# Local/global attention with routed experts: where an even block leaves, when weights split, how list entries are sent

## The chip, the cores and the metric

The kernel runs on one core of one Trainium2 chip. The metric is the device time of one execution in microseconds (us). TensorE multiplies, VectorE and ScalarE work element by element and read PSUM, GpSimd works on SBUF alone and issues the indirect DMAs, SyncE issues the other DMAs. In rows of the profile these are PE (PEld: its weight loads), DVE, ACT, POOL and SP.

## The reference

```python
s_g  = scale * q_g @ k_all.T                   # 32 global queries see all 544 keys
s_ll = where(|i - j| <= 32, scale * q_l @ k_l.T, -1e9)
s_l  = concat([scale * q_l @ k_g.T, s_ll])     # local: 32 global keys and a window
attn = concat([softmax(s_g) @ v_all, softmax(s_l) @ v_all])     # 8 batches, 8 heads, 544 x 64
x    = attn.transpose(0, 2, 1, 3).reshape(4608, 512)
on   = x @ w_skip > 0                          # rows that are computed
e    = argmax(x @ w_gate); gate = softmax(x @ w_gate)[e]        # one of 8 experts for each
out  = x; out[on] = x + gate * (relu(x @ w1[e]) @ w2[e])        # w1 512x1024, w2 1024x512
```

## The kernel before

The attention runs over 32 units (`for u in range(NU + 2)`, L822), each one batch and one pair of heads, 64 queries to a block and eight blocks to a unit. Work on a unit is spread over three turns of the loop: `cur` has its scores and probabilities, `prev` (one turn later) its transposes, `old` (two turns later) its values. `ORDER` (L787) is a list written by hand: it sets the order in which every turn issues its steps, and so the order on each engine, since each engine runs what it is given in order. A unit multiplies scores in two halves (`scores`, L377), reduces and exponentiates them (`probs`, L389: VectorE writes minus the row's maximum to a column of `nmx`, ScalarE the exponential), transposes them (`turn`, `turned`), multiplies by the values (`values`, L511) and copies the result out of PSUM into `xT` in two steps, odd blocks and even blocks (`leave`, L548, both on ScalarE). The bank of the even blocks is the one that the transpose of the global probabilities (`turn_pg`, L479, the tile `psgL`) takes next, in every second unit. Before that transpose GpSimd scales the global probabilities (`scale_g`, L458).

Finished rows are turned back and written out (`rows_turn`, `rows`), and the router's logits are made from them. `route` (L653) turns the logits of two batches (of one batch for batches 6 and 7) into places in eight expert lists: a list of small steps, of which some are fixed to VectorE and seven go to the engine `eng`. They are appended to `stages`, and each `seam` in `ORDER` runs one of them (two from unit 28 on). One step, `counts` (L671), is done by TensorE; one empty step stands ahead of it. When the stages of a list are done, its entries are put into `sends`: each is an indirect DMA from GpSimd that writes 128 entries of 8 bytes (`send`, L716), eight or nine for a pair of batches. `some_sends` (L912) issues two at the end of each unit, four in units 29 and 30; in unit 30 four of the seams issue one more each, and at its end `after` (L901) issues what is left and reads back the first expert's list, from which `first_x` (L866) gathers rows in unit 31.

Beside this the first expert's weights are loaded in eight pieces and split into a high and a low part in sixteen steps (`split_mid`, L892; each a ScalarE copy and a GpSimd subtraction), in units 4, 5, 7, 9, 11, 12, 13, 15 and so on, up to unit 28. The first piece is requested in unit 3, each next one at every second split.

After the attention the eight experts run one after the other (`ffn`, `ffn_half`), in full precision by three products of high and low parts; nothing of that is changed.

Of the kernel before, what the change touches and what calls it, by code (L numbers as in the profile page):

```python
# [10 lines left out]
F32 = mybir.dt.float32  # L11
# [8 lines left out]
P = 128  # L20
B, H, SL, SG, D = 8, 8, 512, 32, 64
# [7 lines left out]
QB = 64  # L29
# [10 lines left out]
LINE = 16  # L40
# [4 lines left out]
def kernel(  # L45
# [12 lines left out]
    nc = tc.nc  # L58
# [67 lines left out]
    sends, stages = [], []  # L126
# [6 lines left out]
    def send_some(n):  # L133
        for _ in range(n):
            if sends:
                sends.pop(0)()
# [83 lines left out]
    with ExitStack() as actx:  # L220
# [3 lines left out]
        st = actx.enter_context(tc.tile_pool(name="st", bufs=1))  # L224
# [20 lines left out]
        smg = [st.tile([P, 640], F32, name=f"smg{i}") for i in range(2)]  # L245
        sumt = [st.tile([P, NP, NB], F32, name=f"sumt{i}") for i in range(2)]
        invt = [st.tile([P, 4, H], F32, name=f"invt{i}") for i in range(2)]
        sumgt = [st.tile([P, 2], F32, name=f"sumgt{i}") for i in range(2)]
        def grid(m):
            return m[:, 0:KW].rearrange("p (r f m) -> p r f m", r=4, f=2)  # L250
# [109 lines left out]
        def pair(u):  # L360

            b, p = divmod(u, NP)
# [3 lines left out]
            nmx = sm.tile([P, NB], F32, name="nmx")  # L366
# [181 lines left out]
            def leave(odd):  # L548
                x4 = xT[b][:, p, :].rearrange("d (j a q) -> d a j q", a=2, q=QB)
                pvi = pvs[odd][:, 0:384].rearrange("d (j r) -> d j r", r=96)  # L550
                nc.scalar.copy(x4[:, odd], pvi[:, :, 0:QB])

            def gather_g():
                nc.vector.reduce_sum(
# [3 lines left out]
                )  # L558

            return SimpleNamespace(  # L560
                u=u, scores=scores, probs=probs, window_g=window_g,
                window_min=window_min, scores_g=scores_g, probs_g=probs_g, normal_g=normal_g,
                scale_g=scale_g, turn=turn, turned=turned, turn_pg=turn_pg, turned_pg=turned_pg,
                turn_g=turn_g, values=values, values_g=values_g, leave=leave, gather_g=gather_g,
# [88 lines left out]
        def route(bs, lg, T, eng):  # L653
            def small(name, dt=F32, e=True):
                if len(bs) > 1:
                    return wk.tile([P, 9, E] if e else [P, 9], dt, name=name + "2")[:, 0:T]
                return rt.tile([P, 5, E] if e else [P, 5], dt, name=name, bufs=2)[:, 0:T]

            mx, se, do, slot = (small(n, e=False) for n in ("mx", "se", "do", "slot"))
            ex, oh, pos = (small(n) for n in ("ex", "oh", "pos"))  # L660
            ohb = small("ohb", BF16)
            slu = small("slu", U32, e=False)
            f8 = first8.unsqueeze(1).to_broadcast([P, T, E])

            def over(a):
                return a.unsqueeze(2).to_broadcast([P, T, E])

            pc = {}
            n = T * E

            def counts():  # L671
                pt = pc[0] = ps_s("pp")
                ohf = ohb.rearrange("p t e -> p (t e)")
                nc.tensor.matmul(pt[:, 0:n], tri, ohf, start=True, stop=False)
                for s in range(1, T):
                    nc.tensor.matmul(
                        pt[:, s * E:n], ones, ohf[:, 0:n - s * E], start=False, stop=s == T - 1
                    )
                for s in range(T):
                    nc.tensor.matmul(  # L680
                        pt[:, n:n + E], ones, ohb[:, s, :], start=s == 0, stop=s == T - 1
                    )

            l8 = lg[:, :, 0:E]
            def weight():
                for j, b in enumerate(bs):
                    t = slice(4 * j, 4 * j + (5 if b % 4 == 3 else 4))
                    nc.vector.reciprocal(dat[:, b, 0:t.stop - t.start, 1], se[:, t])

            steps = [  # L690
                lambda: nc.vector.reduce_max(mx, l8, axis=AX.X),
                lambda: eng.tensor_sub(ex, l8, over(mx)),
                lambda: nc.scalar.activation(ex, ex, AF.Exp),
                lambda: nc.vector.tensor_tensor(oh, l8, over(mx), ALU.is_equal),
                lambda: eng.tensor_single_scalar(do, lg[:, :, E], 0.0, ALU.is_gt),
                lambda: eng.tensor_mul(oh, oh, f8),
                lambda: nc.vector.reduce_max(mx, oh, axis=AX.X),
                lambda: nc.vector.tensor_tensor(oh, over(mx), f8, ALU.is_equal),
                lambda: eng.tensor_mul(ohb, oh, over(do)),
                lambda: nc.vector.reduce_sum(se, ex, axis=AX.X),  # L700
                lambda: eng.tensor_scalar(do, do, -BIG, BIG, ALU.mult, ALU.add),
                lambda: eng.tensor_scalar_add(se, se, 1.0e-9),
                lambda: None,
                counts,
                lambda: nc.vector.tensor_add(
                    pos, pc[0][:, 0:n].rearrange("p (t e) -> p t e", e=E),
                    base.unsqueeze(1).to_broadcast([P, T, E]),
                ),
                lambda: nc.vector.tensor_add(base, pc[0][:, n:n + E], base),
                lambda: eng.tensor_mul(pos, pos, ohb),  # L710
                weight,
                lambda: nc.vector.reduce_sum(slot, pos, axis=AX.X),
                lambda: nc.vector.tensor_add(slu, slot, do),  # L713
            ]

            def send(t):  # L716
                j = min(t // 4, len(bs) - 1)
                ins = nc.gpsimd.indirect_dma_start(  # L718
                    out=lst, out_offset=bass.IndirectOffsetOnAxis(ap=slu[:, t:t + 1], axis=0),
                    in_=dat[:, bs[j], t - 4 * j, :], in_offset=None,  # L720
                    bounds_check=E * CAP - 1, oob_is_err=False,
                )
                apart(ins, "slots", "slots")

            return steps, send

        lgb, lgs, lgw, xrs = {}, {}, {}, {}
        LK = 0

        def batch_rows(b, k, halves=(0, 1)):  # L730
            T = 5 if b % 4 == 3 else 4
            whole = b < B - 1
            bs = (b,) if b >= B - 2 else (b - b % 2, b - b % 2 + 1)
# [32 lines left out]
            if k == T - 1 and halves[-1] == 1:  # L766
                if T == 5:
                    ts_ = slice(4 if whole else 0, 5)
                    stages.append(lambda: nc.vector.reduce_sum(
                        lgs[b][:, ts_], lgb[b][:, ts_].rearrange("p t a e -> p t e a"), axis=AX.X  # L770
                    ))
                if b != bs[-1]:
                    return
                T += t0
                steps, send = route(
                    bs, lgw[bs[0]][:, 0:T], T, nc.vector if b >= B - 2 else nc.gpsimd
                )
                stages.extend(steps)
                if b == B - 3:
                    stages.append(  # L780
                        lambda: nc.vector.tensor_scalar_max(base[:, 0:1], base[:, 0:1], float(GRP))
                    )
                stages.append(lambda: sends.extend([lambda t=t: send(t) for t in range(T)]))
# [3 lines left out]
        ORDER = [  # L787
            "cur.scores 0", "prev.turn_g 0", "loads_pair", "loads_v", "loads_g", "old.turned 1",
            "old.values_g", "cur.probs 0", "cur.scores 1", "inverse", "seam", "old.values 0", "cur.probs 1",
            "cur.window_g", "prev.normal_g", "cur.probs 2", "cur.scores_g", "seam", "prev.scale_g", "split_mid",  # L790
            "old.values 1", "old.leave 1", "cur.window_min", "old.gather_g", "first_x",
            "old.leave 0", "prev.turn 0", "cur.probs 3", "rows", "seam",
            "prev.turn_pg", "setup_late", "seam", "setup", "rows_leave", "seam", "prev.turn_g 1",
            "seam", "cur.probs_g", "prev.turned_pg", "late_rows",
            "prev.turned 0", "prev.turn 1", "last_x", "seam", "sends", "after",
            "last_sends", "split",
        ]
        NU = B * NP
# [3 lines left out]
        with tc.manual_schedule(engines=engines):  # L802
# [18 lines left out]
            prev, old, first = None, None, slice(0, 1)  # L821
            for u in range(NU + 2):  # L822
                cur = pair(u) if u < NU else None

                nth = iter(range(8))
# [64 lines left out]
                        weights[0].load()  # L890

                def split_mid():  # L892
                    if u >= 4 and (u % 4 in (1, 3) or u % 8 == 4):
                        split_one()

                def split_one():
# [12 lines left out]
                    if u == NU - 1:  # L909
                        send_some(len(sends))  # L910

                def some_sends():  # L912
                    if u < NU - 1:
                        send_some(2 if u < NU - 3 else 4)

                loose = dict(
                    loads_g=loads_g, loads_pair=loads_pair, loads_v=loads_v,
                    rows=early_rows, rows_leave=rows_leave, inverse=inverses, late_rows=late_rows, first_x=first_x, setup=setup,
                    setup_late=setup_late, split=split, after=after, seam=seam, sends=some_sends,
                    last_sends=last_sends, split_mid=split_mid, last_x=last_x,  # L920
                )
                for step in ORDER:
                    name, _, arg = step.partition(" ")
# [3 lines left out]
                    who, name = name.split(".")  # L927
# [6 lines left out]
                prev, old = cur, prev  # L934
# [270 lines left out]
```

## Time and profile before

| | us |
|---|---|
| median of 3 runs | 501.85 (501.26 to 502.66) |
| the profiled execution | 500.4 |
| its span, first to last instruction | 498.7 |
| TensorE busy | 451.9 (91%) |
| VectorE, ScalarE, GpSimd busy | 301.8, 278.8, 158.0 |

The first 245 us are the attention, the rest are the experts. Times in rows are us from the start of the span. A row of a window gives its length, then the busy time of each engine with its count of instructions, then TensorE's granted clock as a share of full speed and the share of time in which the DMA engines were busy. A row of the timeline gives start, duration, engine, line, operation and, in brackets, the idle time of the engine before it and what ended it. A row of the waits gives who waited, for whom, us in total, how often, and the longest.

### The profile page before, as it was taken

The numbers are of one execution on the slowest core, as the hardware profiler recorded it, in microseconds if no ns is written. First come the engines' busy times: TensorE is split into PE (matmuls) and PEld (weight loads), VectorE is DVE, ScalarE is ACT, GpSimd is POOL, SyncE is SP. The second block draws the span as 40 slices with busy tenths as digits, with TensorE's granted clock in tenths as the row PEclk, the third lists the DMA queues.
The fourth block names the chain that finished last, engine by engine and source line by source line (L and its number), as shares of the span: only waits on it lengthen the run. The fifth ranks groups of instructions, "written<-read, shape, count | busy, mean of one in ns | idle before, by whom it ended". The sixth has DMA issues, their size and how long they took to land. (4 is left out here: it accounts for less than half of the span.)

```text
span 498.7 us, 13380 instructions
## 1 busy us (share of the span) xinstructions
PE 451.9 (91%) x4962; PEld 376.4 (75%) x4962; DVE 301.8 (61%) x1125; ACT 278.8 (56%) x871; POOL 158.0 (32%) x182
## 2 busy tenths in 40 slices
PE   7969999997989988879798999999999999999991
PEld 3757777776767766648696979898978989799981
DVE  7856888885767876657463229384714747247520
ACT  5859899986878867536441207263524545245400
POOL 6212223345333334635556014223101340023200
PEclk9999999999999999879999999999999999999997
DMA  8796998989887797421235507483910939117100
GB/s 265 248 321 228 338 302 239 333 242 194 274 250 246 208 287 244 135 43 46 90 104 119 210 26 258 159 282 135 322 67 10 346 121 341 48 40 283 47 16 17
DMA packets 50625, 93.31 MB, mean 187 GB/s; under 512 B 15677, under 2 KB 20029, under 8 KB 50529
## 3 DMA queue, kind: packets, MB, share of 16 engines
q1 hardware_dynamic: 44416, 80.78, 50.8%
q0 software_dynamic: 6112, 11.30, 6.7%
q8 instruction: 55, 0.90, 0.8%
q14 instruction: 42, 0.34, 0.2%
HBM read 82.91 MB, written 14.67 MB: 196 GB/s over the span
## 5 line engine op out<-in xcount | busy, mean ns | idle before, releaser
L401 ACT ACTIVATE prob<-prob,nmx 128x160 f32<-128x160 f32 x256 | 106.9, 422 | 24.3 <-DVE nmx L396 22.8
L969 ACT ACTIVATE hh<-ph 128x256 fp32r<-128x256 f32 x72 | 27.7, 385 | 73.4 <-PE ph L964 60.8
L383 PE MATMUL pss<-ks,qs 64*64 64x160 f32 x1024 | 56.2, 310 | 3.9 <-issue 2.8
L980 PE MATMUL py<-w2h,hh 128*128 128x512 f32 x144 | 56.7, 394 | 0.0
L980 PE MATMUL py<-w2h,hlw 128*128 128x512 f32 x144 | 56.3, 391 | 0.0
L980 PE MATMUL py<-w2l,hh 128*128 128x512 f32 x144 | 56.2, 390 | 0.0
L530 PEld LDWEIGHTS pv<-ptT,vw 128*64 128x64 f32 x1024 | 43.7, 143 | 14.3 <-issue 12.9
L1046 POOL DMA_INDIRECT out_dram<-yo,six x12 | 12.2, 1017 | 126.1 <-DVE yo L1045 108.5
L530 PE MATMUL pv<-ptT,vw 128*64 128x64 f32 (+1 forms) x1024 | 49.1, 243 | 2.9 <-issue 2.2
L964 PE MATMUL ph<-xh,w1h 128*128 128x256 f32 x288 | 46.4, 284 | 3.0 <-DVE xl L214 1.0
L401 ACT ACTIVATION_READ_ACCUMULATOR prob<-prob,nmx 128x1 f32 x256 | 49.0, 192 | 0.0
L383 PEld LDWEIGHTS pss<-ks,qs 64*64 64x64 f32 x1024 | 37.4, 135 | 13.1 <-issue 8.8
L964 PE MATMUL ph<-xh,w1l 128*128 128x256 f32 x288 | 45.7, 281 | 0.0
L964 PE MATMUL ph<-xl,w1h 128*128 128x256 f32 x288 | 45.7, 281 | 0.0
L459 POOL TENSOR_TENSOR probg<-probg,ing 128x640 f32<-128x640 f32 x16 | 20.0, 1252 | 79.4 <-ACT prob L401 32.3
L970 DVE SCALAR_TENSOR_TENSOR hlw<-ph,hh 128x256 fp32r<-128x256 f32 x72 | 30.2, 421 | 22.5 <-ACT hh L969 20.0
L964 PEld LDWEIGHTS ph<-xh,w1h 128*128 128x128 f32 x288 | 39.3, 190 | 5.3 <-issue 4.0
L718 POOL DMA_INDIRECT lst<-dat,slu x34 | 35.5, 1043 | 23.1 <-DVE slu L713 9.1
L467 PE MATMUL pst<-ident,prob 128*128 128x128 f32 x256 | 39.8, 281 | 0.0
L964 PEld LDWEIGHTS ph<-xl,w1h 128*128 128x128 f32 x288 | 39.0, 189 | 0.0
L964 PEld LDWEIGHTS ph<-xh,w1l 128*128 128x128 f32 x288 | 39.0, 189 | 0.0
L213 ACT CAST xh<-xt 128x512 fp32r<-128x512 f32 (+1 forms) x22 | 11.1, 550 | 49.3 <-PE xt L206 47.6
(179 smaller groups left out, 945.8 us busy)
## 6 DMA issues: line engine op xcount, KB each, us to landing
raw<-in_w_dram SPq DMA_DIRECT2D x58, 512.0 KB
vw<-in_v_dram SPq DMA_DIRECT2D x32, 512.0 KB
ks<-in_kT_dram SPq DMA_DIRECT2D x32, 400.0 KB
out_dram<-xr SPq DMA_DIRECT2D x32, 256.0 KB
qs<-in_qT_dram SPq DMA_DIRECT2D x31, 256.0 KB
raw<-in_w_dram POOLq DMA_DIRECT2D x6, 512.0 KB
vgs<-in_vgl_dram SPq DMA_DIRECT2D x32, 64.0 KB
lst<-dat,slu POOLq DMA_INDIRECT x34
```

What stands on the lines that cost most here:

```text
L213: nc.scalar.copy(xh[:, c:c + step, ts_], p3[:, c:c + step])
L383: nc.tensor.matmul(banks[odd][head(h ^ odd), j * W:(j + 1) * W], q[head(h), w * QB:(w + 1) * QB], window(k[head(h)], w), start=True, stop= ...
L401: nc.scalar.activation(pt[:, i, :], pt[:, i, :], AF.Exp, bias=nmx[:, i:i + 1], scale=-1.0, accum_out=sums[:, i:i + 1],)
L459: nc.gpsimd.tensor_mul(pg, pg, pgTs["ing"].to_broadcast([P, 640]))
L467: nc.tensor.transpose(pst[:, i * P:(i + 1) * P], pt[:, 4 * hf + i, 0:KW], ident)
L530: nc.tensor.matmul(pv[head(h), j * 96:j * 96 + n], vv[:, w, head(h)], ptT[:, w, h ^ odd, 0:n], start=False, stop=j == 3, skip_group_check= ...
L718: ins = nc.gpsimd.indirect_dma_start(out=lst, out_offset=bass.IndirectOffsetOnAxis(ap=slu[:, t:t + 1], axis=0), in_=dat[:, bs[j], t - 4 * ...
L964: nc.tensor.matmul(ph[:, 0:GRP], hl[a][:, c, f * P:(f + 1) * P], bb[:, c, :], start=i == 0, stop=i == 3 * NC - 1,)
L969: nc.scalar.activation(hh[:, f, :], ph[:, 0:GRP], AF.Relu)
L970: nc.vector.scalar_tensor_tensor(hlw[:, f, :], ph[:, 0:GRP], 0.0, hh[:, f, :].bitcast(F32), ALU.max, ALU.subtract,)
L980: nc.tensor.matmul(py, a[:, f, ts_], hl[bb][:, f, :], start=f == 0 and i == 0, stop=f == NF - 1 and i == 2,)
L1046: ins = nc.gpsimd.indirect_dma_start(out=out, out_offset=bass.IndirectOffsetOnAxis(ap=sidx, axis=0), in_=yo, in_offset=None, bounds_check= ...
```

## The change

- `leave`: the odd blocks stay on ScalarE, the even blocks are copied by VectorE.
- `split_mid` begins at unit 5 in place of 4: sixteen splits still, so the last one comes in unit 29, and each request for a next piece moves with its split.
- Sends of a unit: in place of two (four) at the unit's end, one (two) after `prev.normal_g` and one (two) at the end, each with a GpSimd copy of a column of `nmx` ahead of it (column 0, written by the unit's first reduction, and column 6, written by one of its last two). The seams' own sends in unit 30 and later stay.
- `route`: batches 4 and 5 have `eng` VectorE, as 6 and 7 had.
- Three empty steps ahead of `counts` in place of one, but for batch 7.

```diff
+        pace = st.tile([P, LINE], F32, name="pace")[:, 0:1]
...
-                nc.scalar.copy(x4[:, odd], pvi[:, :, 0:QB])
+                (nc.scalar.copy if odd else nc.vector.tensor_copy)(x4[:, odd], pvi[:, :, 0:QB])
...
-                lambda: None,
+                *[lambda: None] * (1 if bs[0] == B - 1 else 3),
                 counts,
...
-                    bs, lgw[bs[0]][:, 0:T], T, nc.vector if b >= B - 2 else nc.gpsimd
+                    bs, lgw[bs[0]][:, 0:T], T, nc.vector if b >= B - 4 else nc.gpsimd
...
-            "cur.window_g", "prev.normal_g", "cur.probs 2", "cur.scores_g", "seam", "prev.scale_g", "split_mid",
+            "cur.window_g", "prev.normal_g", "sends_1", "cur.probs 2", "cur.scores_g", "seam", "prev.scale_g", "split_mid",
...
-            "prev.turned 0", "prev.turn 1", "last_x", "seam", "sends", "after",
+            "prev.turned 0", "prev.turn 1", "last_x", "seam", "sends_2", "after",
...
-                    if u >= 4 and (u % 4 in (1, 3) or u % 8 == 4):
+                    if u >= 5 and (u % 4 in (1, 3) or u % 8 == 4):
...
-                def some_sends():
-                    if u < NU - 1:
-                        send_some(2 if u < NU - 3 else 4)
+                def paced_sends(i):
+                    for _ in range(1 if u < NU - 3 else 2):
+                        if sends and u < NU - 1:
+                            nc.gpsimd.tensor_copy(pace, cur.nmx[:, i:i + 1])
+                            send_some(1)
```

## Rows read from the trace of the kernel before

**Rows 1.** The page: busy time of the engines, and the granted clock in 40 slices.

```profile
PE 451.9 (91%) x4962; PEld 376.4 (75%) x4962; DVE 301.8 (61%) x1125; ACT 278.8 (56%) x871; POOL 158.0 (32%) x182
...
PEclk9999999999999999879999999999999999999997
```

**Rows 2.** Windows of units 5, 7, 10, 18, 20, 24, 26, 28 to 30; units 6 to 17.

```profile
32.66:41.89 9.23, 6.75 (x99) 5.49 (x98) 3.87 (x24) 7.28 (x28) 3.47 (x3) 0.82 1.02 399
48.55:54.11 5.56, 5.29 (x102) 4.60 (x101) 4.59 (x27) 5.52 (x22) 2.19 (x2) 1.00 0.94 286
66.34:73.22 6.88, 6.88 (x113) 4.70 (x112) 5.38 (x29) 5.85 (x24) 0.34 (x1) 1.00 0.92 292
116.28:127.06 10.78, 8.37 (x114) 5.53 (x113) 5.54 (x29) 5.96 (x24) 4.26 (x5) 1.00 0.78 186
132.62:139.66 7.04, 6.26 (x105) 4.93 (x104) 4.57 (x27) 5.92 (x24) 3.58 (x4) 1.00 0.95 238
162.32:167.83 5.51, 5.51 (x105) 4.48 (x104) 4.87 (x33) 4.65 (x20) 1.06 (x3) 1.00 0.72 226
176.51:184.81 8.30, 6.89 (x105) 4.96 (x105) 5.02 (x26) 4.59 (x19) 2.71 (x3) 1.00 0.99 265
191.29:197.16 5.87, 5.63 (x102) 4.36 (x101) 5.17 (x30) 3.08 (x12) 1.88 (x3) 1.00 0.59 170
197.16:210.86 13.70, 10.26 (x142) 8.38 (x141) 7.48 (x39) 8.79 (x34) 8.38 (x13) 0.88 0.49 162
210.86:224.80 13.94, 10.74 (x109) 6.78 (x109) 8.45 (x40) 4.37 (x19) 4.54 (x5) 0.76 0.26 59
...
41.89:116.28 74.39, 72.00 (x1284) 57.10 (x1283) 60.67 (x324) 67.00 (x264) 20.52 (x23) 1.00 0.87 270
```

**Rows 3.** The waits over the whole span: us in total, times, longest.

```profile
ACT w1h L188 <- DMA raw<-in_w_dram: 4.9, 1, 4.9
...
PE psgL L484 <- ACT xT L551: 3.7, 11, 0.4
...
PE pv L542 <- ACT xT L551: 3.4, 2, 2.1
...
PE pv L542 <- DVE se L700: 2.8, 1, 2.8
DVE mx L697 <- POOL oh L696: 2.6, 1, 2.6
```

**Rows 4.** Groups of instructions by line and shape: busy us, mean ns; idle before, releaser.

```profile
L474 DVE COPY ptT<-pst 128x512 f32<-128x512 f32 x32 | 21.9, 683 | 2.6 <-PE xt L206 2.5
...
L551 ACT COPY xT<-pv 128x256 f32<-128x256 f32 x64 | 20.5, 368 | 10.5 <-PE pv L530 5.1 <-PE xt L206 4.5 <-DVE xTg L554 0.8
...
L495 DVE COPY ptT<-psgL 128x128 f32<-128x128 f32 x16 | 4.4, 274 | 4.8 <-PE psgL L484 4.5
...
L694 DVE TENSOR_TENSOR oh<-lg,mx 128x64 f32<-128x64 f32 x2 | 0.4, 222 | 0.0
...
L674 PE MATMUL pp<-ohb,tri 128*128 128x64 bf16 x2 | 0.4, 203 | 0.6 <-DVE pgT L502 0.6
```

**Rows 5.** The timeline of GpSimd: sends, first and last of four; first of unit 20's two.

```profile
116.77 1.01 POOL L718 DMA_INDIRECT lst<-dat,slu  x1 [0.16 <-issue]
...
120.64 0.97 POOL L718 DMA_INDIRECT lst<-dat,slu  x1 [0.30 <-issue]
...
133.11 1.01 POOL L718 DMA_INDIRECT lst<-dat,slu  x1 [0.16 <-issue]
```

**Rows 6.** The timeline of TensorE in unit 18: first and last of four gaps.

```profile
119.59 0.19 PE L521 MATMUL pv<-ptT,vw 128*64 128x32 f32 x1 [0.48 <-issue]
...
122.53 0.47 PE L530 MATMUL pv<-ptT,vw 128*64 128x96 f32 x6 [1.03 <-issue]
```

**Rows 7.** The timeline in unit 31: GpSimd's scaling, and a VectorE product beside it.

```profile
228.26 1.25 POOL L459 TENSOR_TENSOR probg<-probg,ing 128x640 f32<-128x640 f32 x1 [11.64 <-ACT prob L401]
...
228.47 1.08 DVE L710 TENSOR_TENSOR pos<-pos,ohb 128x32 f32<-128x32 f32 x1
```

More of the change, by code (lines that the diff above doesn't have):

```diff
@@ L560, in pair @@
             return SimpleNamespace(
-                u=u, scores=scores, probs=probs, window_g=window_g,
+                u=u, nmx=nmx, scores=scores, probs=probs, window_g=window_g,
                 window_min=window_min, scores_g=scores_g, probs_g=probs_g, normal_g=normal_g,
@@ L918 @@
                     rows=early_rows, rows_leave=rows_leave, inverse=inverses, late_rows=late_rows, first_x=first_x, setup=setup,
-                    setup_late=setup_late, split=split, after=after, seam=seam, sends=some_sends,
+                    setup_late=setup_late, split=split, after=after, seam=seam, sends_1=lambda: paced_sends(0), sends_2=lambda: paced_sends(6),
                     last_sends=last_sends, split_mid=split_mid, last_x=last_x,
```

## The prediction

> **What bounds the kernel now.** I read the page first: TensorE is busy for 91% of the span, and its granted clock is whole but for two of the 40 slices, near 200 to 225 us [rows 1]. Then windows cut at the start of each unit's first score product, since a share over the span hides which units are long. In units 6 to 17 TensorE is busy for 72.00 of 74.39 us: there it is the bound, and only 2.4 us are to be had, whatever another engine does [rows 2]. Like units repeat to a few hundredths (24, as 8, 12 and 16: 5.51), so that a long one stands out: unit 5 has 9.23 where 7 has 5.56, 18 has 10.78 where 10 has 6.88, 20 has 7.04 and 26 has 8.30 where 24 has 5.51, and 29 and 30 have 27.64 together, at a clock of 0.88 and 0.76 [rows 2]. Last the waits and the timeline, for what those units wait for. After the attention TensorE runs with hardly a gap, on work that isn't touched; what the attention gives reaches the end as long as the list and the gathers behind it come no later, relative to it. So the sum is over attention units.
>
> **The split, a unit later.** In unit 4 ScalarE waits 4.9 us for the first weight piece, still on its way, and behind that split on ScalarE stand the copies out of PSUM for which TensorE then waits 2.1 us [rows 3]. The clock falls after that gap: 0.82 over unit 5 is (1 - 0.82) x 9.23 = 1.7 us of TensorE's work [rows 2]. 2.1 + 1.7 = 3.8 agrees with 9.23 - 5.56 = 3.7. A unit later the piece has landed (the wait ended in what was unit 5), and the split has its place in unit 5 as in 7. Gain: 2.1 (the wait alone) to 3.7; I take 3.5. The second piece's request moves too, behind the loads of unit 7 on SyncE, so those come sooner if anything. The sixteenth split lands in unit 29, among ScalarE's 8.79 us of work there [rows 2]: 0 to 0.6 (half of a whole unit's slack), taken as 0.3 lost.
>
> **The even blocks on VectorE.** ScalarE loses 32 copies of 368 ns, 11.8 us. VectorE gets 32: between its copies of 128x128 in 274 and 128x512 in 683 ns, 1.07 ns an element of a row, so 0.41 us each, 13.1 us [rows 4]. On TensorE's path lies the release of one bank: `psgL` waits for the copy on ScalarE eleven times, 3.7 us in all [rows 3]. ScalarE comes to it only after its exponentials; VectorE makes what those wait for, so it runs ahead of them and reaches the copy earlier. What covers the added 0.41: VectorE idles 74.39 - 60.67 = 13.7 us in twelve units, 1.14 a unit [rows 2], mostly waiting for TensorE. Where a chain on VectorE is next in line (the units with the logits' step), the wait comes back. Gain 0 to 3.7, taken as half, 1.9. Unit 28 has only 0.7 idle on VectorE and also gets the route's steps: 0.3 lost.
>
> **Single sends.** Gaps of TensorE that end on nothing but its own issue lie, in the attention, inside runs of sends. Four sends run from 116.77 to 121.6 without a pause, since GpSimd, with nothing of unit 18 ahead of them, runs through two units' worth [rows 5]; from 119.59 to 122.53 TensorE gets only a few products at a time, four gaps [rows 6]. Excess by windows: 10.78 - 6.88 = 3.9 for unit 18; 7.04 - 5.51 = 1.5 for 20 (two sends); 8.30 - 5.51 = 2.8 for 26, of which I leave 0.6 to its extra block of rows (an estimate: four more transposes), 2.2; 5.87 - 5.51 = 0.4 for 28 (two sends) [rows 2]. In all 8.0. It rises faster than the count, so spacing should pay. But the pacing isn't even: in odd units the scaling and the split stand on GpSimd ahead of the second send, which so slips to the next unit's start, right before that unit's first. Of seventeen sends four pairs remain, at 0.4 each (unit 28's) 1.6. The copy adds a wait on VectorE's reductions to GpSimd's queue: behind it stand the send, the scaling (1.25 us [rows 7]) and the split, and TensorE waits for the scaling alone; the column is written early, so 0.4 in all. Net 6.0. Low end: four pairs as dear as unit 20's leave 8.0 - 6.1 = 1.9, high end 8.0. A loss would need a lone send to cost more than the pair of unit 28.
>
> On instruction supply the Trainium skill speaks against this gain. Its page "Runtime: NRT & Kernel Launch", section "Instruction fetch mechanics", says that TensorE holds some 2048 instructions, refilled in large blocks over a queue of its own and mostly hidden. By it a run of 5 us can't starve it, and the gaps have another cause; by the rows they lie inside the runs [rows 5, 6]. No row shows the store itself. It makes the first rival.
>
> **Routing 4 and 5 on VectorE, counts later.** In unit 29 VectorE waits 2.6 us for GpSimd's part of a route step, which stands there behind a split, and TensorE 2.8 us for what VectorE does next [rows 3]; the clock loss is 0.12 x 13.7 = 1.6 us [rows 2]. Now VectorE does these steps itself: seven of about 0.22 us (the like product, [rows 4]), 1.6 us, of which five stand ahead of the transposes that TensorE wants: 1.0 of the wait stays. One product beside GpSimd's scaling took 1.08 in place of some 0.2 us and ended with it [rows 7]; one or two such meetings would add 0.9 each. The page "SBUF — State Buffer", section on the three doors, has a rule for it: an operation of VectorE with two SBUF inputs and one of GpSimd shut each other out for a whole instruction. The trace agrees with 1.08. By it alone three of the moved steps could be held, 2.6 us more.
>
> The empty steps keep TensorE from reaching `counts` before its input: 0.6 [rows 4]. So unit 29: 2.8 - 1.0 + 1.6 + 0.6 = 4.0, low end 1.4 with three steps held. Unit 30 holds the eight sends of this list in one run. It can't fall under VectorE's 8.45 + 0.41 [rows 2], a gain of 5.1 at most. Of its sends only four get a copy ahead; the seams' four don't, so that I count runs of three and five. Taken: half, 2.5; low end 0. Together 6.5 (1.4 to 9.1).
>
> **Behind it.** `counts` of batch 6 moves to the seam right behind the second scores of unit 31, whose bank VectorE must free first: up to 0.6. The last of the eight sends leaves later in unit 30, the first list is read back after it, and in unit 31 the index cast stands on VectorE ahead of the even copy: up to 1.4. Taken: 0.8 lost (0 to 2.0).
>
> **Sum.** 3.5 - 0.3 + 1.9 - 0.3 + 6.0 + 6.5 - 0.8 = 16.5. The profiled execution took 500.4 us, 1.45 under the median: 483.9 against it, 485.3 as a median. With all low ends: 2.1 - 0.6 + 0 - 0.3 + 1.9 + 1.4 - 2.0 = 2.5, or 499.3; with all high ends 3.7 + 3.7 - 0.3 + 8.0 + 9.1 = 24.2, or 477.6.
>
> **Rivals.** First: the spacing doesn't take hold, or TensorE's gaps aren't the runs' doing. Then the 6.0 and unit 30's 2.5 go: 485.3 + 8.5 = 493.8. For it: the cause is inferred from where the gaps lie, and pairs and a run of five remain. Against: no such gap lies in units 6 to 15, where nothing is sent and DMA is as busy (0.87 [rows 2]). 0.25.
>
> Second, slower: VectorE becomes the bound. The place is the even copy, ahead of the last two reductions of a unit, on which the next unit's products hang. If all 32 lie whole on the path, 13.1; if the 16 in odd units also meet the scaling and are held 0.86 each as the product was [rows 7], 13.8 more. 26.9 against the other gains, 16.5 - 1.9 = 14.6: 12.3 slower, 514.2. It decides where a copy costs TensorE more than 14.6 / 32 = 0.46 us. Against: 1.14 us idle a unit, and the copies out of PSUM average 683 ns over 32 [rows 4], many of them beside GpSimd. 0.08.
>
> Third, no change to speak of: the low ends come together, with the first list late in unit 31 and the clock down once more: about 500.5. 0.05.
>
> **How the numbers follow.** The forecast has 0.62, with a range of its own from 479 to 491. 478 to 497 also takes in the first rival, and leaves out the second, the third and the far ends. Faster by over 0.3% (1.5 us, about what a measurement of this kernel can tell): 0.62 + 0.25 = 0.87. Same 0.05, slower 0.08.
>
> **What would show it.** Unit 5 near 5.6 us at full clock, no wait of ScalarE for a piece; no `psgL` wait on ScalarE, and VectorE's copies near 0.41; units 18 and 26 near 7.3 and 6.5; a copy of GpSimd before each send and no four sends in a run before unit 29; units 29 and 30 near 9.7 and 11.4 with the clock whole. Wrong if TensorE's issue gaps go with each lone send, if `psgL` or the score products wait on VectorE, or if the cast of the first list waits for its DMA.

## The result

The changed kernel takes 486.20 us (median of four runs, 485.47 to 486.56) where the kernel before takes 501.56 (four runs, 499.67 to 502.66): a ratio of 0.9696, 95% interval 0.9664 to 0.9728. The forecast was 485.3. The profiled execution took 486.03 us against 500.4, a span of 484.3 against 498.7.

The page of the changed kernel, the two lines that answer to [rows 1]:

```profile
PE 448.4 (93%) x4962; PEld 375.5 (78%) x4962; DVE 311.6 (64%) x1164; ACT 270.6 (56%) x839; POOL 159.0 (33%) x196
...
PEclk9899999999999999979999999999999999999997
```

ScalarE has 32 operations fewer, VectorE 39 more, GpSimd 14 more, and the span is 14.4 us shorter. Where, is read from windows of the changed kernel, as in [rows 2]: units 5, 10, 18, 20, 26, 27, 29, 30, then from unit 31 to the first expert product, then units 6 to 17 (start:end, length, busy time of TensorE, its weight loads, VectorE, ScalarE and GpSimd, granted clock, DMA share, GB/s).

```profile
31.44:36.19 4.75, 4.75 (x98) 4.17 (x98) 4.06 (x25) 4.75 (x20) 1.37 (x2) 1.00 1.01 394
60.53:67.98 7.45, 6.96 (x114) 4.66 (x113) 6.28 (x31) 5.90 (x25) 0.91 (x1) 1.00 0.98 329
110.74:117.81 7.07, 7.07 (x114) 4.89 (x113) 5.56 (x28) 5.09 (x23) 3.85 (x7) 1.00 0.92 279
123.74:130.16 6.42, 6.41 (x105) 4.85 (x104) 4.88 (x29) 5.33 (x21) 3.52 (x6) 1.00 1.03 280
166.75:172.26 5.51, 5.51 (x106) 4.48 (x105) 2.99 (x19) 3.29 (x14) 2.35 (x4) 1.00 0.91 314
172.26:180.87 8.61, 6.50 (x107) 5.24 (x106) 7.14 (x36) 7.29 (x28) 4.25 (x6) 1.00 0.91 270
185.94:198.11 12.17, 9.62 (x143) 7.21 (x142) 10.90 (x53) 8.73 (x33) 7.16 (x9) 1.00 0.52 159
198.11:204.27 6.16, 5.85 (x102) 4.28 (x101) 4.61 (x24) 3.28 (x14) 3.50 (x7) 1.00 0.62 182
204.27:230.54 26.27, 21.30 (x266) 17.88 (x266) 14.94 (x75) 12.75 (x42) 15.63 (x19) 0.87 0.09 22
...
36.19:110.74 74.55, 72.44 (x1284) 57.98 (x1283) 64.47 (x337) 64.74 (x257) 21.77 (x25) 1.00 0.90 292
```

Cut by stretches, with the terms of the forecast beside them (before, the first expert product starts at 245.65):

| stretch | before | after | gained | forecast |
|---|---|---|---|---|
| up to unit 6 | 41.89 | 36.19 | 5.7 | 3.5 (split) |
| units 6 to 17 | 74.39 | 74.55 | -0.2 | most of 1.9 (leaves) |
| units 18 to 28 | 80.88 | 75.20 | 5.7 | 6.0 (sends) - 0.3 |
| unit 29 | 13.70 | 12.17 | 1.5 | 4.0 - 0.3 |
| unit 30 | 13.94 | 6.16 | 7.8 | 2.5 |
| unit 31 to the first expert product | 20.85 | 26.27 | -5.4 | -0.8 |
| the experts, to the end | 253.0 | 253.8 | -0.7 | 0 |

The sum is 14.4, against 16.5. But the last four lines show that the total came closer than its terms.

What TensorE waits for in the changed kernel, over the span (us in total, times, longest), to be read beside [rows 3]:

```profile
PE psgT L484 <- POOL probg L460: 4.9, 5, 2.2
PE pss L384 <- issue: 2.8, 5, 1.1
PE pv L543 <- DVE se L701: 2.3, 1, 2.3
```

The waits of `psgL` and of `pv` on ScalarE's copy of `xT` are gone, and in the attention ScalarE no longer waits for a weight piece. What is late next is GpSimd's scaling of `probg`.

### The profile page after: what moved, and what is told of

Read it like the earlier page. It is cut to its first block, busy times and chain, and to the rows that moved or that the text cites. A ratio compares the mean times of both kernels' runs of the same rounds, so it can differ in the third digit from the quotient of the medians.

```text
span 484.3 us, 13432 instructions
## 1 busy us (share of the span) xinstructions
PE 448.4 (93%) x4962; PEld 375.5 (78%) x4962; DVE 311.6 (64%) x1164; ACT 270.6 (56%) x839; POOL 159.0 (33%) x196
## 5 line engine op out<-in xcount | busy, mean ns | idle before, releaser
L384 PE MATMUL pss<-ks,qs 64*64 64x160 f32 x1024 | 57.5, 313 | 3.7 <-issue 2.8
L531 PEld LDWEIGHTS pv<-ptT,vw 128*64 128x64 f32 x1024 | 42.5, 140 | 10.9 <-issue 8.3
L213 ACT CAST xh<-xt 128x512 fp32r<-128x512 f32 (+1 forms) x22 | 11.2, 551 | 48.1 <-PE xt L206 38.9
```

The lines of the kernel that those rows point to most:

```text
L384: nc.tensor.matmul(banks[odd][head(h ^ odd), j * W:(j + 1) * W], q[head(h), w * QB:(w + 1) * QB], window(k[head(h)], w), start=True, stop= ...
L531: nc.tensor.matmul(pv[head(h), j * 96:j * 96 + n], vv[:, w, head(h)], ptT[:, w, h ^ odd, 0:n], start=False, stop=j == 3, skip_group_check= ...
```

## The experiments

The twelve kernels ran in four groups, each beside its own runs of the kernel before. In two groups that took 500.15 and 500.48 us; in the two others it took 481.84 and 483.89, and the chip does not decide it: the first, the third and the fourth group (500.15, 500.48 and 483.89) ran on the same one, the second on another. The kernel before took 501.56 beside the result, so that one belongs to the first kind. I call the two the 500 and the 482 condition. Ratios are compared only within a group; a gain given behind a ratio is what the ratio, which is one of means, makes of the median before (for the first three parts the medians themselves differ by 2.3, 4.1 and 9.6 us). What sets a condition is open (below).

### Each part alone (500 condition, before 500.15)

**The split alone.**

```diff
-                    if u >= 4 and (u % 4 in (1, 3) or u % 8 == 4):
+                    if u >= 5 and (u % 4 in (1, 3) or u % 8 == 4):
```

> The kernel before with the split moved by a unit and nothing else. Theory: the split in unit 4 cost unit 5 both its gap and half a clock, and its second weight request also held up the keys that unit 4 waits for; unit 5 falls from 9.2 to about 5, unit 4 from 7.3 to about 5.7, in all 5 to 6 us faster (496). Rival: only the gap and the clock of unit 5 are the split's, 3.5 us (498), and unit 4's wait for its keys stays at 1.9; its absence in the changed kernel then has another cause.

Measured 497.86 us, ratio 0.9944 (0.9915 to 0.9973): 2.8 us, nearer the rival's 3.5 than the 5 to 6 of the theory.

**The even blocks alone.**

```diff
-                nc.scalar.copy(x4[:, odd], pvi[:, :, 0:QB])
+                (nc.scalar.copy if odd else nc.vector.tensor_copy)(x4[:, odd], pvi[:, :, 0:QB])
```

> The kernel before with the even blocks on VectorE and nothing else. Theory: the wait of psgL goes from ScalarE, but the units after the logits' step lose about as much to VectorE, so 0.3 to 1.5 us faster (501). Rival: the whole wait of 3.7 us is gained (498). Rival on the other side: VectorE is on the path and each copy costs, slower by 3 us or more.

Measured 496.02 us, ratio 0.9916 (0.9889 to 0.9942): 4.2 us, the rival's case and a little more than the full `psgL` wait. Units 4 and 5, first with the split alone, then with the leaves alone:

```profile
25.99:31.78 5.79, 5.39 (x101) 4.29 (x100) 5.33 (x30) 4.85 (x21) 0.00 (x0) 1.00 0.87 281
31.78:37.62 5.84, 4.97 (x99) 4.15 (x98) 3.68 (x24) 5.84 (x25) 2.19 (x2) 1.00 1.03 408
```

```profile
26.42:32.01 5.59, 5.41 (x102) 4.30 (x101) 5.50 (x32) 4.02 (x18) 0.00 (x0) 1.00 0.91 300
32.01:39.06 7.05, 5.28 (x98) 4.39 (x97) 4.14 (x25) 5.56 (x22) 2.53 (x2) 1.00 1.03 412
```

Before, these two units take 7.34 + 9.23 = 16.57 us. The split alone makes them 11.63, the leaves alone 12.64, both together 10.43 (5.68 and 4.75). But 16.57 is the longest of its kind: in four other profiles with the same code up to there (the sends alone, the route alone, and twice without sends) the two units take 14.5 to 15.6, while unit 6 begins at 41.3 to 41.7 in all four, near the 41.89 of before. So the start of unit 6 is the surer measure: 37.62 with the split alone, 39.06 with the leaves alone, 36.19 with both. Against 41.89 they gain 4.3 and 2.8 alone and 5.7 together, less than their sum: both free the same copies, those that stood on ScalarE behind a split that waited for its piece. In units 6 to 15 the leaves alone gain 0.1 us (62.22 to 62.10).

**The paced single sends alone.**

```diff
-                def some_sends():
-                    if u < NU - 1:
-                        send_some(2 if u < NU - 3 else 4)
+                def paced_sends(i):
+                    for _ in range(1 if u < NU - 3 else 2):
+                        if sends and u < NU - 1:
+                            nc.gpsimd.tensor_copy(pace, cur.nmx[:, i:i + 1])
+                            send_some(1)
```

> The kernel before with the single, paced sends and nothing else. Theory: units 18, 20 and 26 lose about 7 us of excess, units 17, 19, 25 and 27 give back some 2.5 us because the scaling on GpSimd stands behind a send that waits for VectorE; the last list still goes out in two runs and moves its stall to unit 31, 0 to 3 us gained there. Together 5 to 8 us faster (495). Rival: TensorE's gaps don't come from runs of sends, then within 1.5 us of before.

Measured 490.6 us, ratio 0.9824 (0.979 to 0.9859): 8.8 us, the largest part. Windows of units 18, 27, 29, 30 and from 31 to the first expert product:

```profile
115.67:122.66 6.99, 6.99 (x114) 4.76 (x113) 5.19 (x27) 5.31 (x24) 3.82 (x7) 1.00 1.10 210
...
177.56:185.76 8.20, 6.50 (x107) 5.24 (x106) 6.40 (x33) 7.63 (x30) 4.23 (x6) 1.00 1.00 320
190.83:204.74 13.91, 10.32 (x142) 8.45 (x141) 8.33 (x43) 8.95 (x34) 8.60 (x15) 0.88 0.49 159
204.74:211.21 6.47, 5.92 (x110) 4.49 (x109) 6.30 (x37) 3.29 (x14) 2.34 (x4) 1.00 0.82 124
211.21:236.34 25.13, 20.91 (x260) 17.32 (x258) 12.81 (x60) 14.08 (x46) 15.75 (x19) 0.86 0.10 24
```

Unit 18 falls from 10.78 to 6.99. Unit 27 grows from 6.48 to 8.20, and what unit 30 gains (13.94 to 6.47) is given back by half in unit 31 (20.85 to 25.13). All three also stand in the changed kernel: they come with the pacing.

**The route on VectorE and the empty steps alone.**

```diff
-                lambda: None,
+                *[lambda: None] * (1 if bs[0] == B - 1 else 3),
...
-                    bs, lgw[bs[0]][:, 0:T], T, nc.vector if b >= B - 2 else nc.gpsimd
+                    bs, lgw[bs[0]][:, 0:T], T, nc.vector if b >= B - 4 else nc.gpsimd
```

> The kernel before with batches 4 and 5 routed by VectorE and the two more empty steps, nothing else. Theory: unit 29 keeps about 2 us of TensorE's wait (VectorE does the steps itself, one of them held beside GpSimd's split), gains 1 to 3 us; the run of eight sends and its stall in unit 30 stay: 1 to 4 us faster (499). Rival: the 7.8 us that unit 30 gained in the changed kernel came from the routing and not from the sends: 8 us or more faster (493).

Measured 500.34 us, ratio 0.9997 (0.9976 to 1.0017): nothing. The theory's 1 to 4 us did not come, and neither did the rival's 8. It does gain 2.0 in unit 29 (13.70 to 11.69, clock whole) and 0.7 behind unit 30. But the empty steps lie in the other lists' routing too: units 16 and 24, 5.51 us in all three other single parts, take 6.05 here and in the changed kernel. Unit 27 grows to 7.56. Unit 18 takes 12.19 (clock 0.86) in place of 10.78, but that is not this part's doing: with the split alone it takes 11.92 and with the leaves alone 12.24, so with its run of four sends unit 18 takes 10.78 to 12.24, from profile to profile.

### Are TensorE's gaps the sends' doing?

**Without the sends of the first six batches**, once in each group of the 482 condition.

```diff
-                stages.append(lambda: sends.extend([lambda t=t: send(t) for t in range(T)]))
+                if bs[0] >= B - 2:
+                    stages.append(lambda: sends.extend([lambda t=t: send(t) for t in range(T)]))
```

> The kernel before without the 25 sends of batches 0 to 5, so the expert lists hold only batches 6 and 7; routing, counting and the experts' products stay. Theory: the long units are long because of the sends: 18 near 6.9, 20 near 5.5, 26 near 6, 30 near 8 us, no issue gaps of TensorE in them, the clock whole in unit 30; about 8 us in units 16 to 28 and 5 to 6 in 30 and 31, 13 us faster (488). Rival: the gaps come from elsewhere (instruction supply at these places of the program) and stay: within 2 us of before.

> The kernel before without the sends of the first six batches, once more, for a place where before takes near 500 us (its lists hold the last two batches only, so its output differs). Theory (where before takes near 500 the sends hold TensorE up, and that is the whole difference between the two conditions): units 18, 20, 26 and 28 take 6.9, 5.5, 5.5 and 5.1 us, units 30 and 31 together 24 to 26 in place of 34.8, and the kernel takes about 481 us, ratio 0.962. Rival (most of the difference lies elsewhere, and the gaps move on to other instructions): 490 us or more. Where before takes near 482, both expect the ratio 0.995 of the earlier run.

Measured 479.53 us beside 481.84, ratio 0.9953 (0.9919 to 0.9986), and 480.55 beside 483.89, ratio 0.9924 (0.989 to 0.9958). So in the 482 condition the sends of before cost 2 to 4 us in all, as little as the rival of the first run had said; the units are as short as its theory had them. The second of these runs, units 18, 26, 30 and 31 to the first expert product:

```profile
116.12:123.01 6.89, 6.89 (x114) 4.66 (x113) 5.39 (x29) 5.87 (x24) 0.34 (x1) 1.00 0.70 215
170.92:176.43 5.51, 5.51 (x106) 4.48 (x105) 4.74 (x26) 4.51 (x19) 0.00 (x0) 1.00 0.94 299
201.29:207.31 6.02, 5.71 (x109) 4.49 (x109) 5.85 (x36) 4.22 (x19) 0.00 (x0) 1.00 0.33 127
207.31:225.62 18.31, 16.78 (x260) 14.77 (x258) 13.11 (x60) 12.86 (x43) 12.10 (x14) 1.00 0.03 3
```

The same units take 10.78, 8.30, 13.94 and 20.85 us in the profile of before. Over units 18 to 31 before is 19.9 us longer than this (129.37 against 109.50), and it is 17 to 18 us longer in the 500 condition than in the 482 condition. Where nothing is sent the two profiles agree: units 6 to 17, 19 and 21 to 25 differ by 0.02 us at most. All this fits "the sends hold TensorE up in the one condition only, and that is the difference". The direct measurement, this kernel in the 500 condition, did not come about, so the difference itself is argued and not shown.

**Dummy sends in quiet units**, one run in each condition.

```diff
+                def dose():
+                    n = {8: 1, 10: 2, 12: 4}.get(u, 0)
+                    if n or u == 6:
+                        nc.gpsimd.tensor_copy(pace, cur.nmx[:, 0:1])
+                    for _ in range(n):
+                        nc.gpsimd.indirect_dma_start(
+                            out=dums.pop(), out_offset=bass.IndirectOffsetOnAxis(ap=dumx, axis=0),
+                            in_=dumv, in_offset=None, bounds_check=NT - 1, oob_is_err=False,
+                        )
+                    for _ in range(20 if u == 6 else 0):
+                        nc.gpsimd.tensor_copy(pace, cur.nmx[:, 0:1])
```

> The changed kernel with more put into units without sends: in unit 6 twenty small GpSimd copies and no DMA (some 4 us of GpSimd), in unit 8 one indirect DMA like a send to a table of its own, in unit 10 two in a run, in unit 12 four in a run. Theory: the loss rises faster than the count: unit 6 unchanged (7.15), 8 at most 0.2 over 5.67, 10 0.3 to 0.7 over 7.45, 12 with its successor 2.5 to 4 over 5.67, with issue gaps of TensorE in 12. Rival: each DMA costs the same, 0.5 to 1 us, so 8 loses 0.5 to 1, 10 twice and 12 four times that. Rival: it is GpSimd's work as such, then unit 6 loses as much as unit 12.

> The changed kernel with GpSimd work added in units where nothing is sent: twenty copies of one column in unit 6, one dummy indirect DMA in unit 8, two in unit 10, four in unit 12. Theory (a run of indirect DMAs holds TensorE's issue up, more for each further one, where before takes near 500): unit 6 stays at 7.15 us, unit 8 at 5.67 or up to 0.3 more, unit 10 goes from 7.45 to 7.9 or more, unit 12 from 5.67 to 8 or 9; where before takes near 482, all four stay. Rival (TensorE's gaps come from GpSimd's being busy as such, or from what surrounds the real sends): unit 6 grows with its twenty copies, or unit 12 stays within 0.3 of 5.67 where before takes near 500.

In the 482 condition 476.83 us (one run, before 481.84), in the 500 condition 493.79 (one run; the changed kernel beside it 483.83). Units 6, 8, 10, 12, 13 and 14 in the 500 condition:

```profile
36.31:43.45 7.14, 7.13 (x113) 4.79 (x112) 5.17 (x26) 6.04 (x26) 5.05 (x22) 1.00 1.04 385
48.54:54.21 5.67, 5.67 (x105) 4.64 (x105) 4.95 (x30) 5.31 (x24) 2.23 (x3) 1.00 0.98 325
60.65:68.22 7.57, 7.08 (x113) 4.78 (x112) 6.10 (x29) 5.63 (x25) 3.10 (x4) 1.00 1.10 330
73.30:81.30 8.00, 6.38 (x105) 4.76 (x104) 4.27 (x26) 4.86 (x20) 6.15 (x7) 1.00 0.86 323
81.30:88.05 6.75, 6.61 (x106) 5.42 (x105) 6.25 (x32) 6.03 (x23) 1.91 (x3) 1.00 0.75 42
88.05:101.15 13.10, 9.94 (x113) 6.67 (x112) 6.85 (x33) 6.24 (x26) 2.17 (x6) 0.74 0.90 313
```

and units 12 to 14 of the same kernel in the 482 condition:

```profile
73.03:78.69 5.66, 5.66 (x106) 4.63 (x105) 4.86 (x30) 5.32 (x24) 3.96 (x5) 1.00 1.01 375
78.69:84.84 6.15, 6.02 (x106) 5.21 (x105) 5.57 (x28) 5.28 (x21) 3.94 (x5) 1.00 1.09 234
84.84:92.41 7.57, 6.96 (x113) 4.65 (x112) 6.64 (x33) 6.13 (x26) 2.17 (x6) 1.00 0.90 204
```

Twenty GpSimd copies and a lone send cost nothing in either condition, a pair 0.1 us (7.45 to 7.57) in the 500 condition. Four in a run cost 2.3 in their own unit (5.67 to 8.00), with TensorE gaps that end on its own issue as in [rows 6], 0.6 in the next and 5.5 in the one after that, where one gap of 3.2 us is followed by 6.83 us at half clock, though nothing is sent there. In the 482 condition the same four cost nothing. So a run of indirect DMAs can hold TensorE up, far more than in proportion to its length, but only in one condition. By GpSimd's being busy alone it isn't explained. Each dose is one profile; its units 7, 9 and 11, without a dose, repeat the changed kernel's to 0.01 us, so that 0.1 can be read.

The same trace shows what the gap of 3.2 us waits for. The gap, and the queue of the DMA records that is named instruction:

```profile
91.84 0.54 PE L389 MATMUL pss<-ks,qs 64*64 64x160 f32 x4 [3.17 <-issue]
```

```profile
q8 instruction: 55, 0.90, 0.8%
```

This queue's 55 packets are blocks of 16384 bytes; in the attention one comes for about every 125 products of TensorE, in all profiles, so I take them for its instructions (the records don't name the engine). The tenth block starts when TensorE has begun 1216 to 1244 products, in all thirteen other profiles. Here it starts at 89.40 us, with 1342 begun, and product 1342 is the one that TensorE stands before from 88.67 to 91.84. By the other profiles it was due between 77.5 and 82.5 us; in unit 13, from 81.30 on, single packets of another queue took up to 5.0 us. So this gap is a late block, by the trace; no run tests it. The short gaps are not: those of the kernel before in unit 18 lie at products 1822 to 1832, between a block that had landed at 115.57 and a next one that starts with 1847 products begun, no later than in other profiles (1841 to 1895). What holds TensorE up in those stays open.

### The changed kernel again, and two variants

**The changed kernel, unchanged** (500 condition, before 500.48).

> The changed kernel once more, beside other kernels, because the kernel before took 500.2 us in the first group of runs and 481.8 in the second. Theory (the sends hold TensorE up only in one of the two conditions, and nearly all the rest is equal): where before takes near 500 the ratio is 0.970 (486 us); where before takes near 482 about 6 us are gained, ratio 0.988 (476 us). Rival (the second condition is faster for a reason that has nothing to do with the sends): the ratio is 0.970 in both, 467 us beside 482.

Measured 483.83 us, ratio 0.9657 (0.9587 to 0.9727): in the 500 condition the gain comes again. In the 482 condition the changed kernel itself was not run; its two near relatives there (the dummy sends, and the next variant) gain about 5 and 6 us.

**The first send behind the scaling.**

```diff
-            "cur.window_g", "prev.normal_g", "sends_1", "cur.probs 2", "cur.scores_g", "seam", "prev.scale_g", "split_mid",
+            "cur.window_g", "prev.normal_g", "cur.probs 2", "cur.scores_g", "seam", "prev.scale_g", "sends_1", "split_mid",
```

> The changed kernel with the unit's first send issued behind the scaling in place of ahead of it. Theory: TensorE's waits for the scaling in units 17, 19, 25 and 27 (0.33, 0.63, 0.31 and 1.45 us, 2.7 in all) are the price of the copy's wait on VectorE and go: 2 to 3 us faster than the changed kernel (483.7). Rival: the scaling was late anyway because VectorE was late, then within 1 us of it (486).

Measured in the 482 condition: 476.13 us, ratio 0.9879 (0.9828 to 0.9929). Without the changed kernel beside it this settles only unit 27: 6.07 us, where the kernel with the dummy sends, which is the changed kernel there, takes 6.93 in the same group.

**The same, with the split of unit 28 in unit 26** (500 condition).

```diff
-                    if u >= 5 and (u % 4 in (1, 3) or u % 8 == 4):
+                    if u >= 5 and (u % 4 in (1, 3) or u in (12, 20, 26)):
```

> The changed kernel with the first of a unit's two sends behind the scaling on GpSimd, and the split of unit 28 moved to unit 26. Theory (the scaling waits behind the paced send, and the split shuts VectorE's product out in unit 29): the waits of 0.3, 0.6, 0.3 and 2.0 us in units 17, 19, 25 and 27 go, and 0.9 in unit 29: 3.5 us faster than the changed kernel beside it. Rival (the sends only slip to the next ones and run as pairs, and unit 29 waits for another step): within 1 us of the changed kernel.

Measured 480.67 us (479.75 to 481.74), ratio 0.961 (0.9543 to 0.9678); all four runs lie under all four of the changed kernel beside it (481.82 to 484.3): 3.2 us faster, the fastest of its group. Units 27, 28 and 29:

```profile
172.60:179.04 6.44, 6.30 (x106) 5.38 (x105) 5.77 (x29) 5.96 (x25) 4.62 (x7) 1.00 0.96 247
179.04:185.94 6.90, 6.06 (x102) 4.84 (x101) 6.69 (x37) 3.76 (x17) 4.06 (x7) 1.00 0.92 269
185.94:195.56 9.62, 9.39 (x142) 7.20 (x142) 8.45 (x43) 7.68 (x29) 4.77 (x6) 1.00 0.65 190
```

Unit 27 takes 8.61 and 7.82 us in the two profiles of the changed kernel, unit 29 12.17 and 12.75: they gain 1.4 to 2.2 and 2.5 to 3.1. The theory's 3.5 us came nearly whole. The rival was half right: the sends slip, and two of them, at 179.89 and 181.30, now make a pair in unit 28, which grows from 5.07 to 6.90 with two gaps of issue.

**The last eight sends spread besides** (500 condition).

```diff
-                        send_some(len(sends))
-                        slots(first, 0)
...
+                def sends_1():
+                    paced_sends(0, 2 if u == NU - 2 else 1)
+                def sends_a():
+                    if u == NU - 2:
+                        paced_sends(2)
+                    if u == NU - 1:
+                        paced_sends(2)
+                        slots(first, 0)
```

> The kernel before this one, with the last eight sends spread besides: six in unit 30 in runs of two at most, two in unit 31, each behind a copy, and the first list is read back behind them. Theory (the run of five is what unit 31 loses): where before takes near 500 unit 31 loses its gaps of 2.3 us and its half clock, 4 to 5 us faster than the one without; where before takes near 482, within 1 us of it. Rival (the list comes later and the first gather with it): 1 to 2 us slower than the one without, in both.

Measured 484.57 us, ratio 0.9706 (0.963 to 0.9781): 3.9 slower than the variant before it, where the theory had 4 to 5 faster and the rival 1 to 2 slower. GpSimd's timeline, the first and the last of six sends in a row, and the first gather:

```profile
198.44 0.98 POOL L719 DMA_INDIRECT lst<-dat,slu  x1 [0.56 <-issue]
...
205.13 0.98 POOL L719 DMA_INDIRECT lst<-dat,slu  x1 [0.16 <-issue]
...
215.39 1.06 POOL L119 DMA_INDIRECT xfirst<-out_dram,six  x1 [3.18 <-DVE six L102]
```

The copies ahead of the sends read columns that VectorE, which runs ahead, had already written: they hold nothing back, and six sends leave at 1.34 us each. Unit 31 to the first expert product takes 30.23 us, with 10.24 us at half clock. Part of the loss is what the rival had named: the last send leaves at 211.18, the first gather starts 4.0 us later than without this change (215.39 against 211.40), and TensorE waits 1.5 us for the even copy on VectorE; how the rest divides is not separated. A wait spaces only while what it waits for is still to come.

## Why the prediction came out

**The split (3.5).** Right in mechanism, with 2.8 us for it alone. What it left out: the leaves take copies out of the same queue. With both, unit 6 begins 5.7 us sooner, of which the prediction had 3.5 under the split; the other 2.2 it had, about, as leaves spread over all units.

**The even blocks (1.9).** VectorE's copies take what was worked out, 0.41 us (one line, both engines: ns least, median, most):

```profile
L552 DVE COPY xT<-pv x32: 412/414/417, 19.3 to 227.8; 128x256 f32<-128x256 f32 x32
L552 ACT COPY xT<-pv x32: 348/366/374, 20.1 to 227.3; 128x256 f32<-128x256 f32 x32
```

The `psgL` wait is gone. But only 1.8 of its 3.7 us lay in units 6 to 17, and there the gain is lost again in the units where the text had suspected it: unit 7 falls by 0.48 (5.56 to 5.08), unit 10, with the logits' step, rises by 0.57 (6.88 to 7.45), and the twelve units together are 0.2 longer. TensorE's waits that are left there are four, 1.8 us in all; that of unit 10, 0.5, ends on a copy of ScalarE, and only one, 0.6, on VectorE. The amount was about right, the place wrong: that is luck. The second rival, VectorE as the bound, would need its copies on the path, and of that these units show little.

**Single sends (6.0).** Units 18 to 28 gain 5.7, in the changed kernel as with the sends alone (5.7 in units 16 to 28). Within the term two errors cancel. What pairs remain cost less than the 1.6 that was taken (unit 26 falls to 5.51, where 6.5 was expected; unit 20, at 6.42, keeps 0.9 over the 5.51 that it takes without sends). The scaling behind a waiting copy, taken at 0.4 in all, costs more: of TensorE's five waits for it, 4.9 us in total, the longest, 2.2, lies in unit 1, where nothing is sent yet, and the other four make 2.7, where the kernel before had 0.6 outside that unit. GpSimd in unit 27 shows how:

```profile
175.79 0.19 POOL L916 COPY pace<-nmx 128x1 f32<-128x1 f32 x1 [4.43 <-DVE nmx L397]
176.54 0.98 POOL L719 DMA_INDIRECT lst<-dat,slu  x1 [0.56 <-issue]
177.53 1.27 POOL L460 TENSOR_TENSOR probg<-probg,ing 128x640 f32<-128x640 f32 x1
```

The copy held GpSimd for 4.43 us, and from its start to the scaling's end pass 3.0 us. "The column is written early" was the step of this term that failed; putting the send behind the scaling gives unit 27 back 1.4 to 2.2 us.

**Unit 29 (4.0).** It gained 1.5. The clock came back whole, but 2.3 us of TensorE's wait stay. VectorE's steps, and the split on GpSimd beside them:

```profile
187.24 1.16 DVE L699 TENSOR_TENSOR oh<-mx,first 128x64 f32<-128x64 f32 x1
188.43 0.22 DVE L700 TENSOR_TENSOR ohb<-oh,do 128x64 bf16<-128x64 f32 x1
```

```profile
187.06 1.26 POOL L189 TENSOR_TENSOR w2l<-raw,w2h 128x512 fp32r<-128x512 f32 x1 [2.94 <-ACT w2h L188]
```

The product ends with the split, as that of [rows 7] did with the scaling. This is one of the "one or two meetings", priced at 0.9 each and left out of the sum. With the split moved away it takes 0.22 and unit 29 9.62 us, near the 9.7 that was forecast. The product in that run, and the one that was held in the run of the route alone:

```profile
185.63 0.22 DVE L699 TENSOR_TENSOR oh<-mx,first 128x64 f32<-128x64 f32 x1
```

```profile
201.65 1.23 DVE L699 TENSOR_TENSOR ohb<-oh,do 128x64 bf16<-128x64 f32 x1
```

The rule of the Trainium skill, page "SBUF — State Buffer", section "SBUF: two separate sides", that an operation of VectorE with two SBUF inputs and one of GpSimd shut each other out for a whole instruction, agrees with 1.16 here, with 1.23 of the next product in the run of the route alone, and with 0.22 where GpSimd was elsewhere. The prediction's low end had three products held by that rule; one was.

**Unit 30 (2.5) and behind it (-0.8).** The two largest misses, which belong together: +7.8 and -5.4. The floor, "it can't fall under VectorE's 8.45 + 0.41", failed: the work is not bound to the unit. Two copies of late rows, 1.38 us, VectorE now does in unit 29, other steps only in unit 31, and unit 30 shows 4.61 us of it. And the stall that the eight sends cause did not get halved but moved. GpSimd's run of five, first and last, and two of TensorE's gaps beside it:

```profile
201.57 0.98 POOL L719 DMA_INDIRECT lst<-dat,slu  x1 [0.56 <-issue]
...
206.75 0.97 POOL L719 DMA_INDIRECT lst<-dat,slu  x1 [0.30 <-issue]
```

```profile
207.35 0.36 PE L384 MATMUL pss<-ks,qs 64*64 64x160 f32 x2 [0.99 <-issue]
208.79 0.54 PE L384 MATMUL pss<-ks,qs 64*64 64x160 f32 x2 [1.08 <-issue]
```

"Runs of three and five" was right; that three of the five would stand in unit 31, and the gaps with them, was missed. There the clock falls to half (1.2 GHz) for 6.83 us from 207.87, which costs (1 - 0.87) x 26.27 = 3.4 us beside the gaps. Taken together, unit 30 and what is behind it gain 2.4 up to the first expert product, where the prediction had 2.5 - 0.8 = 1.7. That the two misses nearly cancel is luck: what was worked out was neither.

**The empty steps.** Priced as a gain in unit 29 alone, they also cost 0.54 each in units 16 and 24, whose lists have them too.

**The first rival** (the gaps aren't the runs' doing) is refuted for the 500 condition by the four dummy sends: 2.3 us in their own unit, 8.5 with the next two. For the 482 condition it is nearer the truth: there is no such gap to remove. The prediction had put this rival on a rule of the Trainium skill, page "Runtime: NRT & Kernel Launch", section "Instruction fetch mechanics": instructions are fetched in large blocks while earlier ones run, and the cost is mostly hidden. The traces agree for the short gaps, whose blocks were not late, and in the 482 condition; the gap of 3.2 us behind the four dummy sends is a block that was not hidden. "No row shows the store itself" was so for the rows read; the DMA records do show the blocks. By their counts TensorE ran dry 98 to 126 products after the block was due, with the weight loads some 200 to 250 instructions and not the 2048 of the prediction.

**The sum.** 16.5 was forecast and 14.4 came. The split, the leaves and the sends together are forecast at 11.1 and came to 11.2; units 29 to the end at 4.0 - 0.3 + 2.5 - 0.8 = 5.4 and came to 3.2. (One small reading: the clock of the kernel before is below full in three of the 40 slices, not two; the third is the last, in the experts.)

## What to carry to other kernels

A wait that is put on an engine to space its transfers delays everything queued behind it; put it behind the work that others wait for, and see that what it waits for is really still to come at that point. Two parts that free the same queue gain less together than apart, so that a sum of single gains overstates them, and a stall that is only spread may come out whole a unit later. Before a gap is put down to a cause, dose the suspected cause in a quiet stretch, and do it wherever the kernel is to run.

## What the runs showed of the hardware

- **One program, two conditions.** The kernel before took 500.48 us in one group of runs and 483.89 in another on the same chip, and each group kept its condition. In the 482 condition the profiles show TensorE waiting on nothing but its own issue for 0.2 us at most, beside runs of four and five sends too; in the 500 condition it is 8.3 us for the kernel before and 4.0 for the changed one. What sets it (where the program or its buffers lie, which core it has) no run here tells apart.
- **Runs of indirect DMAs.** One costs TensorE nothing, two 0.1 us, four 2.3 us and more two units later. In the unit behind the four, the core moved 42 GB/s at a DMA share of 0.75, where the same unit shows 234 GB/s in the 482 condition: the DMA engines were busy and moved little. Single packets took up to 5.0 us there, the block of instructions that was due came late, and TensorE stood for 3.2 us until it had come. Why the engines moved so little stays open.
- **VectorE beside GpSimd.** A product of 0.22 us took 1.16 or 1.23 beside a GpSimd operation of 1.26 us, and ended with it.
